# Four small reorderings at the start, at two hand-overs and in the last product of an attention and two-layer kernel

## Chip, cores and metric

One core of a Trainium2 chip runs the whole program. The metric is the device time of one execution in microseconds (us); a comparison takes the median of the runs of each kernel.

## What is computed

Causal attention over 2 batches, 12 heads, 448 positions and 64 values a head, and then two layers on its 896 x 768 result. Cut to what matters:

```python
scores = scale * q @ k.T ; scores = where(above diagonal, -1e9, scores)
attn = exp(scores - max) / (sum + 1e-9) ; x = attn @ v        # 896 x 768 after the heads are joined
g1 = sigmoid(x @ w_gate) * (x @ w_val)                        # product 1, two 768 x 1536 weights
y = g1 @ w_out                                                # product 2, 1536 x 768
h = y @ w2_in ; g2 = h * clip(h + 3, 0, 6) / 6                # product 3, 768 x 2048
out = g2 @ w2_out                                             # product 4, 2048 x 768
```

Inputs arrive as 64-bit words (weights) and 32-bit words (q, k, v); the result is 32-bit.

## The kernel before

Every factor of the four products is held as two parts, hi (rounded) and lo (what is left), and each product is the sum of three terms hi*hi, hi*lo and lo*hi on TensorE (PE). ScalarE (ACT) makes hi, VectorE (DVE) makes lo by a subtraction. Weights come as 64-bit words in units of 128 x 768: SyncE (SP) fetches them three units ahead, ACT and DVE turn them into 32-bit numbers (L115, L120, L124, L128, L134: "decode") and split them (`dec_hi` L153, `dec_lo` L158).

**Attention** works on 12 pairs of heads. Its steps are sorted by a table of due times (`AT`, `OWN`) in `emit_in_order`, so each engine gets them in that order. `load` (L248) fetches q and k of a pair as two halves of 112 KB each; all of these go through SP's queue but one: k of pair 0, which the line below sends through ACT's queue. In the table that fetch stands behind the turning out of the first transposed q.

```python
(nc.scalar if (p, nm) == (0, "k") else nc.sync).dma_start(
```

`t_pe` (L260) transposes q and k on PE, `t_out` copies them out of PSUM (q by ACT at L270, k by DVE at L272), `s_pe` (L285, L293) makes the scores, `s_max`, `s_exp`, `s_nrm`, `c_pe`, `d_pe` do the rest. 19 idle matmuls (`z_pe`, L456) on constants keep PE at work in the first microseconds; nine of them stand first on PE.

**Products 1 and 3** make their first units (eight and four) plainly with `halves` (L190, 36 matmuls of 448 columns a unit) and the rest by the class `Pairs`: for a pair of weight units it makes seven products P1 to P7 (L708, nine matmuls of 448 columns each) into three PSUM banks instead of eight, with sums of blocks made by DVE (`w_sums`). `run` writes out the order by hand. P1, P6, P7 and P4 add up in one bank (`banks[p][0]`), P5 and then P3 in a second (`banks[p][1]`). Between them ACT copies out what is there (`copy_out`, L725) and DVE adds the rest (`add_out`, L729): P4 may begin only when P7's state of bank 0 has been copied out. For all pairs but the last, P4 and P3 are put between the products of the next pair; for the last pair they stand alone at the end of `run`, P4 first. The hooks `end1` to `end3` split factors for the next product while this goes on. In product 1 the pairs end by sigmoid or a multiplication (L875, L877), in product 3 by hardswish (L1045 on ACT, L1046 on DVE).

**Product 2** (`halves`, L190) makes six blocks `py` of 128 x 896, with two units of weights each. **Product 4** (L1161, 384 columns a matmul) runs over two column halves `c`, eight steps `s` of two factors `g2[f]` (f = 0 to 15) and seven row tiles `t`; the last two steps are done together, row tile by row tile. In the first half `g2_split` splits two factors a step (ACT L1128, DVE L1129), and `advance` decodes and splits one weight unit a step; on DVE they stand in one line.

Of the kernel before, what the change touches and what calls it, by code (L numbers as in the profile page):

```python
# [8 lines left out]
F32 = mybir.dt.float32  # L9
# [22 lines left out]
def kernel(  # L32
# [12 lines left out]
    nc = tc.nc  # L45
    B, H, S, D = q.shape
# [126 lines left out]
    def acc():  # L173

        pool = psum[acc_n[0] // 2 % len(psum)]
        acc_n[0] += 1
        return pool.tile([P, 2, 512], F32, tag="m", name="m")
# [33 lines left out]
    with tc.manual_schedule():  # L211

        with ExitStack() as actx:
# [19 lines left out]
            live = {}  # L233

            def load(p, nm):
                b, hp = divmod(p, NPAIR)
                if nm == "v":
                    for j in range(2):
                        chunks = v[b, 2 * hp + j].rearrange("(c p) d -> p c d", p=D)
                        for x in range(2):  # L240
                            nc.sync.dma_start(
                                out=vs[p % NV][x * D : (x + 1) * D, x != j :, j],
                                in_=chunks[:, x != j :: 2],
                            )
                    return
                t = p_raw.tile([CP, S // CP, 2, D], F32, tag=nm, name=nm)
                for j in range(2):
                    (nc.scalar if (p, nm) == (0, "k") else nc.sync).dma_start(  # L248
                        out=t[:, :, j, :],
                        in_=(q if nm == "q" else k)[b, 2 * hp + j].rearrange(  # L250
                            "(c p) d -> p c d", p=CP
                        ),
                    )
                live[nm, p] = t
# [260 lines left out]
            def emit_in_order():  # L515
# [19 lines left out]
                for key in sorted(left, key=lambda key: (when(key), key)):  # L535
                    _, fn, args = left[key]
                    fn(*args)

            ones = nc.const_aps.tensor(1.0, [P, 512], BF16)
            idle_ps = ps_pt.tile([P, 512], F32, tag="pt", name="pt")  # L540
            make_identity(nc, identf)
# [83 lines left out]
        def w_dec():  # L625

            i = stream[0]
            stream[0] += 1
            u = order[i]
            decode_a(u)  # L630
            if i + 3 < NU:
                load_unit(order[i + 3])
            if u not in in_pairs:
                behind.append(u)

        def w_parts():
            while behind:
                u = behind.pop(0)
                (dec_dma if u < len(order1) else decode_b)(u)
# [4 lines left out]
        class Pairs:  # L644
# [110 lines left out]
            def P7_add(self, p):  # L755
                self.add_out(p, 1, "C22")

            def P4(self, p):
                self.product(self.banks[p][0], self.grp.pop((p, 4)), 0, "T4", False)

# [6 lines left out]
            def run(self, end1, end2, end3):  # L767

                for p in range(self.n):
                    end = p == self.n - 1
                    self.P1(p)
                    self.P1_out(p)
                    if p:
                        self.P7_add(p - 1)
                    if p or not self.ahead:
                        self.w_g1(p + 1)
                        w_dec()  # L780
                    self.P2(p)
                    self.w_g1_lo(p + 1)
                    self.P2_add(p)
                    if p:
                        self.P4(p - 1)
                        self.P4_out(p - 1)
                    self.P6(p)
                    self.P6_out(p)
                    if self.ahead and p == 0:
                        y_split("T4")  # L790
                    self.w_sums(p + 1)
                    if p:
                        self.P3(p - 1)
                        self.P3_add(p - 1)
                    if end:
                        end1()
                    self.w_g4(p + 1)
                    self.w_g2(p + 1)
                    self.P5(p)
                    soon = p and self.soon(p - 1)  # L800
                    if not end:
                        w_parts()
                    if soon:
                        self.finish(p - 1)
                    if not end:
                        w_dec()
                    if p and not soon:
                        self.finish(p - 1)
                    self.P7(p)
                    self.P7_out(p)  # L810
                    if end:
                        self.P7_add(p)
                        end2()
                    else:
                        self.w_g3(p + 1)
                p = self.n - 1
                self.P4(p)
                self.P4_out(p)
                self.P3(p)
                w_parts()  # L820
                end3()
                self.P3_add(p)
                self.finish(p)

        def single_banks():
            for pool in reversed(psum):
# [134 lines left out]
        g1 = {}  # L961
# [33 lines left out]

        for o in range(KD):
            py = acc()
            for s in range(2):
                halves(py, u, g1_of, 6 * s, s == 0, s == 1)
                if s == 1:  # L1000
                    for b in range(2):
                        split(y_of(0, o, b), y_of(1, o, b), py[:, b, :S])
                    if o < HK:
                        nc.scalar.copy(both(yr[o]), py[:, :, :S])
                    else:
                        (y11, y12), (t4, t3) = (
                            [yr[i][:, b * S : (b + 1) * S] for b in range(2)] for i in (o - HK, o)
                        )
                        sub(t3, py[:, 1, :S], y12)
                        sub(y12, y12, y11)  # L1010
                        add(y11, t3, y11)
                        sub(t4, py[:, 0, :S], y11)
                if 2 * o + s in (4, 6):
                    w_dec()
                w_dec()
                w_parts()
                u += 1
# [101 lines left out]
        def g2_split(*fs):  # L1119
            for f in fs:  # L1120
                if f >= K2:
                    continue
                i = 2 * f
                if i < 3 * len(homes2):
                    hi, lo = (home(homes2, i + x, "g2") for x in range(2))
                else:
                    hi, lo = tiles_of_e(i)
                nc.scalar.mul(hi, g2_raw(f), 1.0 / 6.0)  # L1128
                nc.vector.scalar_tensor_tensor(  # L1129
                    lo, g2_raw(f), 1.0 / 6.0, hi.bitcast(F32), op0=ALU.mult, op1=ALU.subtract,  # L1130
                )
                g2[f] = hi, lo
# [10 lines left out]
        third.run(  # L1143
            lambda: g2_split(0), lambda: g2_split(1), lambda: None,
        )
        g2_split(2, 3)
        w_dec()
        w_parts()
        u = stream[0] - 3
# [4 lines left out]
        for c in range(2):  # L1154
            cs = slice(c * HC, (c + 1) * HC)
            po = [None] * NTT

            def block(t, s, w):
                for i in range(2):
                    for n, (a, e) in enumerate(TERMS):  # L1160
                        nc.tensor.matmul(  # L1161
                            po[t],
                            lhsT=g2[2 * s + i][a][:, t * P : (t + 1) * P],
                            rhs=w[e][:, i * HC : (i + 1) * HC],
                            start=(s == 0 and i == 0 and n == 0),
                            stop=(s == NS - 1 and i == 1 and n == 2),
                        )

            osb = acts.tile([P, NTT, HC], F32, tag=f"r1{c}", name="osb")
            for s in range(NS - 2):  # L1170
                if c == 0:
                    g2_split(2 * s + 4, 2 * s + 5)
                for t in range(NTT):
                    if s == 0:
                        if t % 2 == 0:
                            pair = acc()
                        po[t] = pair[:, t % 2, :HC]
                    block(t, s, split_t[u])
                advance(u)
                u += 1  # L1180

            for t in (0, 2, 4, 6, 1, 3, 5):
                for i in range(2):
                    block(t, NS - 2 + i, split_t[u + i])
                if t % 2:
                    nc.vector.tensor_copy(osb[:, t], po[t])
                else:
                    nc.scalar.copy(osb[:, t], po[t])
                if t == 6:
                    advance(u)  # L1190
                if c == 1:
                    nc.sync.dma_start(out=outs[:, t, cs], in_=osb[:, t])
            advance(u + 1)
            u += 2
            if c == 0:
                nc.sync.dma_start(out=outs[:, :, cs], in_=osb)
# [31 lines left out]
```

## Time and profile before

| | us |
|---|---|
| median of three runs | 590.04 (589.8 to 591.88) |
| profiled execution, its own time | 589.66 |
| its span, first to last instruction | 587.9 |
| PE busy | 573.8 (98%) |
| DVE busy | 450.6 (77%) |
| ACT busy | 325.1 (55%) |
| attention, until product 1 has PE alone | 0 to 110 |
| product 1 | 110 to 268 |
| product 2 | 268 to 355 |
| product 3 | 355 to 465 |
| product 4 | 465 to 587 |

Busy time of a matmul includes its way through the array, so matmuls overlap and 98% does not say that PE runs at its peak; the distance between the starts of two matmuls tells the pace. What PE waited for, and where, is told by the table of waits and by the timeline.

### The profile page before, as it was taken

The numbers are of one execution on the slowest core, as the hardware profiler recorded it, in microseconds if no ns is written. First come the engines' busy times: TensorE is split into PE (matmuls) and PEld (weight loads), VectorE is DVE, ScalarE is ACT, GpSimd is POOL, SyncE is SP. The second block draws the span as 40 slices with busy tenths as digits, with TensorE's granted clock in tenths as the row PEclk, the third lists the DMA queues.
The fourth block names the chain that finished last, engine by engine and source line by source line (L and its number), as shares of the span: only waits on it lengthen the run. The fifth ranks groups of instructions, "written<-read, shape, count | busy, mean of one in ns | idle before, by whom it ended". The sixth has DMA issues, their size and how long they took to land.

```text
span 587.9 us, 8611 instructions
## 1 busy us (share of the span) xinstructions
PE 573.8 (98%) x3252; PEld 506.1 (86%) x3253; DVE 450.6 (77%) x673; ACT 325.1 (55%) x619; POOL 88.1 (15%) x146
## 2 busy tenths in 40 slices
PE   6999999999999999999999999999999999999997
PEld 3666666899998999889999999988899899899997
DVE  1778995588778889889767887898999888867601
ACT  1988986454747565577343223777776644433200
POOL 0545455012201111110000000113122000000000
PEclk7999999999999999999999999999999999999999
DMA  7645625069848776761334533577988333338002
GB/s 150 155 118 132 146 67 177 2 157 216 212 131 193 180 208 168 198 180 31 108 115 154 162 107 108 145 179 187 216 191 224 94 107 110 107 109 255 0 3 92
DMA packets 86921, 82.21 MB, mean 140 GB/s; under 512 B 35680, under 2 KB 77408, under 8 KB 86880
## 3 DMA queue, kind: packets, MB, share of 16 engines
q1 hardware_dynamic: 79904, 64.27, 37.0%
q0 software_dynamic: 6048, 17.17, 15.9%
q8 instruction: 25, 0.41, 0.3%
q10 hardware_dynamic: 928, 0.23, 0.2%
q14 instruction: 16, 0.13, 0.1%
HBM read 61.73 MB, written 2.75 MB: 110 GB/s over the span
## 4 chain that ended last, share of the span: by engine, by line
PE 55%; DVE 29%; ACT 10%; issue 4%; DMA 2%; ACTq 0%; DVEq 0%
PE m L1161 17%; PE w L708 11%; PE m L190 10%; DVE b L128 5%; PE pav L367 5%; PE s L293 4%; PE pt L347 4%; DVE b L134 4%; DVE lo L158 3%; DVE b L124 3%; ACT hi L153 2%; ACT b L115 2%; PE tr L260 2%; DVE g L182 2%; DVE raw L120 2%
## 5 line engine op out<-in xcount | busy, mean ns | idle before, releaser
L1161 PE MATMUL m<-hi,g 128*128 128x384 f32 x448 | 114.3, 335 | 0.7 <-DVE g L1129 0.7
L153 ACT CAST hi<-b 128x768 fp32r<-128x768 f32 x36 | 29.8, 836 | 104.3 <-DVE b L134 96.3
L1161 PEld LDWEIGHTS m<-hi,g 128*128 128x128 f32 x448 | 80.8, 188 | 1.5 <-DVE g L1129 1.3
L1161 PE MATMUL m<-lo,g 128*128 128x384 f32 x224 | 74.9, 335 | 0.4 <-DVE lo L158 0.4
L708 PE MATMUL w<-T,hi 128*128 128x448 f32 x252 | 72.0, 367 | 1.4 <-ACT g2r L725 1.4
L190 PE MATMUL m<-g,hi 128*128 128x448 f32 x288 | 70.1, 365 | 0.0
L128 DVE SCALAR_TENSOR_TENSOR b<-b,raw 128x768 int32<-128x768 int32 x68 | 65.3, 960 | 2.3
L134 DVE SCALAR_TENSOR_TENSOR b<-raw,b 128x768 int32<-128x768 int32 x68 | 65.3, 960 | 2.4
L115 ACT ACTIVATE b<-raw 128x768 f32<-128x768 f32 x68 | 61.3, 905 | 0.0
L190 PEld LDWEIGHTS m<-g,hi 128*128 128x128 f32 x288 | 54.1, 188 | 4.3
L124 DVE TENSOR_SCALAR b<-b 128x768 f32<-128x768 f32 x68 | 37.9, 557 | 25.7 <-ACT b L115 25.3
L158 DVE TENSOR_TENSOR lo<-b,hi 128x768 fp32r<-128x768 f32 x36 | 34.2, 956 | 27.4 <-ACT hi L153 27.2
L337 POOL TENSOR_SCALAR pr<-pr,rc 128x192 f32<-128x192 f32 (+3 forms) x96 | 46.1, 497 | 53.0 <-DVE rc L329 43.9
L708 PEld LDWEIGHTS w<-T,hi 128*128 128x128 f32 x252 | 47.1, 188 | 5.9 <-ACT g2r L725 1.8
L190 PE MATMUL m<-x,hi 128*128 128x448 f32 x192 | 49.1, 368 | 0.0
L708 PE MATMUL w<-T,lo 128*128 128x448 f32 x126 | 46.3, 368 | 0.7 <-DMA lo<-S 0.5
L317 ACT ACTIVATE pr<-s,nm 128x192 f32<-128x192 f32 (+3 forms) x96 | 44.5, 476 | 3.7 <-DVE nm L305 3.2
L144 POOL DMA_DIRECT2D lo<-S x26 | 24.9, 956 | 131.4 <-ACT lo L143 111.2
L1161 PEld LDWEIGHTS m<-lo,g 128*128 128x128 f32 x224 | 42.0, 188 | 0.7 <-DVE lo L158 0.7
L305 DVE TENSOR_REDUCE nm<-s 128x2 f32<-128x384 f32 (+3 forms) x48 | 30.7, 681 | 14.9 <-PE s L293 14.5
L190 PE MATMUL m<-g,lo 128*128 128x448 f32 x144 | 41.0, 366 | 0.0
L190 PEld LDWEIGHTS m<-x,hi 128*128 128x128 f32 x192 | 35.7, 188 | 3.1 <-issue 0.4
(127 smaller groups left out, 1054.7 us busy)
## 6 DMA issues: line engine op xcount, KB each, us to landing
raw<-in_moe_w_out_dram SPq DMA_DIRECT2D x28, 768.0 KB, 4.4
raw<-in_moe_w_in_dram SPq DMA_DIRECT2D x16, 768.0 KB, 4.7
lo<-S POOLq DMA_DIRECT2D x26, 384.0 KB, 4.2
raw<-in_moe_w_gate_dram SPq DMA_DIRECT2D x12, 768.0 KB, 5.1
raw<-in_moe_w_val_dram SPq DMA_DIRECT2D x12, 768.0 KB, 5.3
q<-in_q_dram SPq DMA_DIRECT2D x24, 112.0 KB, 2.9
g<-b POOLq DMA_DIRECT2D x7, 384.0 KB, 6.5
k<-in_k_dram SPq DMA_DIRECT2D x22, 112.0 KB, 4.0
```

The lines of the kernel that those rows point to most:

```text
L115: nc.scalar.activation(b, words(u)[0].bitcast(F32), AF.Copy, scale=REBIAS)
L124: nc.vector.tensor_scalar(b, b, UPPER_MAX, -UPPER_MAX, op0=ALU.min, op1=ALU.max)
L128: nc.vector.scalar_tensor_tensor(bi, bi, 3, words(u)[1], op0=ALU.logical_shift_left, op1=ALU.bitwise_or)
L134: nc.vector.scalar_tensor_tensor(bi, words(u)[0], -(2 ** 31), bi, op0=ALU.bitwise_and, op1=ALU.bitwise_or)
L153: nc.scalar.copy(hi, part_t[u])
L158: nc.vector.tensor_sub(lo, part_t.pop(u), split_t[u][0].bitcast(F32))
L190: nc.tensor.matmul(ps[:, b, :S], lhsT=w[a][:, i * P : (i + 1) * P], rhs=x(c, k0 + i, b), start=(first and i == 0 and n == 0), stop=(last a ...
L305: nc.vector.tensor_reduce(nm, live["s", p, t], axis=AX.X, op=ALU.max, negate=True)
L317: nc.scalar.activation(to if j else to[:, ::-1], ps[:, j].rearrange("p (c d) -> p c d", d=D), AF.Exp, bias=nm[:, j : j + 1], accum_out=sm[ ...
L337: nc.gpsimd.tensor_scalar(pr[:, j], pr[:, j], rc[:, j : j + 1], 1.0, op0=ALU.mult, op1=ALU.mult)
L708: nc.tensor.matmul(ps, lhsT=w[a][:, k * P : (k + 1) * P], rhs=x[:, c, i], start=(first and i == 0 and n == 0), stop=(i == HK - 1 and n == ...
L1161: nc.tensor.matmul(po[t], lhsT=g2[2 * s + i][a][:, t * P : (t + 1) * P], rhs=w[e][:, i * HC : (i + 1) * HC], start=(s == 0 and i == 0 and ...
```

## The change

- `load(0, "k")` is called ahead of everything else of the attention, and `load` returns at once where the tile is already there. The two halves of k of pair 0 thus become the first instructions on ACT's queue, ahead of its table load; the step in the table issues nothing any more.
- For the last pair of `run`, a new `P5_out` copies P5 out of bank 1 into C22 ahead of P7, and a new `P5_add` adds bank 0 (P1 + P6 + P7) to it by DVE after P7, in the place of `P7_out` and `P7_add`. P3 then comes ahead of P4, and `P4_out` goes behind `finish`.
- Ahead of the first block of product 2 one 32-bit matmul of 64 x 64 on a factor that is already there writes a corner of `py`, which the next matmul overwrites.
- `g2_split` makes three factors ahead of product 4 instead of two, and its steps of two go on from there.

```diff
             def load(p, nm):
                 b, hp = divmod(p, NPAIR)
+                if (nm, p) in live:
+                    return
...
+            load(0, "k")
             ones = nc.const_aps.tensor(1.0, [P, 512], BF16)
...
+            def P5_out(self, p):
+                nc.scalar.copy(self.hold(p, "C22"), self.banks[p][1])
+
+            def P5_add(self, p):
+                self.add_out(p, 0, "C22")
...
+                    if end:
+                        self.P5_out(p)
                     self.P7(p)
-                    self.P7_out(p)
                     if end:
-                        self.P7_add(p)
+                        self.P5_add(p)
                         end2()
                     else:
+                        self.P7_out(p)
                         self.w_g3(p + 1)
                 p = self.n - 1
-                self.P4(p)
-                self.P4_out(p)
                 self.P3(p)
                 w_parts()
                 end3()
                 self.P3_add(p)
+                self.P4(p)
                 self.finish(p)
+                self.P4_out(p)
...
             py = acc()
+            if o == 0:
+                t = g1[0][0].bitcast(F32)[:, :D]
+                nc.tensor.matmul(py[:D, 0, :D], lhsT=t, rhs=t, start=True, stop=True)
...
-        g2_split(2, 3)
+        g2_split(2, 3, 4)
...
-                    g2_split(2 * s + 4, 2 * s + 5)
+                    g2_split(2 * s + 5, 2 * s + 6)
```

ACT's first rows, before:

```order
L270 ACT_TABLE_LOAD
L270 ACTIVATE qt<-tr 128x448
L248 DMA k<-in_k_dram 112x4x64 x2
L270 ACTIVATE qt<-tr 128x448
L317 ACTIVATE pr,sm<-s,nm 128x3x64
```

The same rows now:

```order
L250 DMA k<-in_k_dram 112x4x64 x2
L272 ACT_TABLE_LOAD
L272 ACTIVATE qt<-tr 128x448 x2
L319 ACTIVATE pr,sm<-s,nm 128x3x64
L319 ACTIVATE pr,sm<-s,nm 128x192
```

The fetch of k moved from behind the copy of the transposed q, which waits for PE, to the front of the queue.

PE at the end of product 1, before (T_1723 is P7's factor, T_1724 P4's, x_73 P3's; `m` is product 2):

```order
L708 MATMUL w<-T_1723,lo 128x448
L708 MATMUL w<-T_1724,g 128x448 x9
L708 MATMUL w<-x_73,hi 128x448 x2
L708 MATMUL w<-x_73,lo 128x448
L190 MATMUL m<-g_2963,hi 128x448 x4
```

The same place now, from P7's last matmul:

```order
L711 MATMUL w<-T_1723,lo 128x448
L711 MATMUL w<-x_73,hi 128x448 x2
L711 MATMUL w<-x_73,lo 128x448
L711 MATMUL w<-T_1724,g 128x448 x9
L1011 MATMUL m<-g_2963 64x64
L190 MATMUL m<-g_2963,hi 128x448 x4
```

P3 stands between P7 and P4 now (its six rows of two and one matmuls are cut to the first two), and the 32-bit matmul stands ahead of product 2. The end of product 3 changes in the same way, without that matmul.

DVE from the last add of P7 or P5 in product 3 to the first decode of product 4, before (w_4526 to w_4528 are the last pair's banks, g2r_4538 and 4539 its C blocks):

```order
L729 TENSOR_TENSOR g2r_4539<-w_4527,g2r_4539 128x448
L1129 SCALAR_TENSOR_TENSOR g2_4621<-g2r_3751,g2_4592 128x896
L1046 SCALAR_TENSOR_TENSOR g2r_4539<-h_4633,w_4526 128x448
L158 TENSOR_TENSOR lo_4647<-b_4497,hi_4645 128x768
L158 TENSOR_TENSOR lo_4651<-b_4542,hi_4649 128x768
L729 TENSOR_TENSOR g2r_4538<-w_4527,g2r_4538 128x448
L1046 SCALAR_TENSOR_TENSOR g2r_4539<-h_4654,g2r_4539 128x448
L1046 SCALAR_TENSOR_TENSOR g2r_4538<-t_4657,g2r_4538 128x896
L1129 SCALAR_TENSOR_TENSOR g2_4621<-g2r_3751,g2_4621 128x896
L1129 SCALAR_TENSOR_TENSOR g2_4662<-g2r_3946,g2_4662 128x896
L120 TENSOR_SCALAR raw_4432<-raw_4432 128x768
```

And now (numbers one or two higher):

```order
L732 TENSOR_TENSOR g2r_4540<-w_4527,g2r_4540 128x448
L1143 SCALAR_TENSOR_TENSOR g2_4622<-g2r_3752,g2_4593 128x896
L158 TENSOR_TENSOR lo_4636<-b_4498,hi_4634 128x768
L158 TENSOR_TENSOR lo_4640<-b_4543,hi_4638 128x768
L732 TENSOR_TENSOR g2r_4539<-w_4528,g2r_4539 128x448
L1060 SCALAR_TENSOR_TENSOR g2r_4540<-h_4652,g2r_4540 128x448
L1060 SCALAR_TENSOR_TENSOR g2r_4539<-t_4655,g2r_4539 128x896
L1060 SCALAR_TENSOR_TENSOR g2r_4540<-h_4658,w_4527 128x448
L1143 SCALAR_TENSOR_TENSOR g2_4622<-g2r_3752,g2_4622 128x896
L1143 SCALAR_TENSOR_TENSOR g2_4663<-g2r_3947,g2_4663 128x896
L1143 SCALAR_TENSOR_TENSOR g2_4666<-g2r_3947,g2_4663 128x896
L120 TENSOR_SCALAR raw_4433<-raw_4433 128x768
```

P4's hardswish moved from the third place to the eighth, and a third split stands ahead of the decode; in the last step of the first half of product 4 one split is left where there were two.

## Rows read from the trace of the kernel before

**Rows 1.** The page: busy us of each engine, share of the span, instructions.

```profile
PE 573.8 (98%) x3252; PEld 506.1 (86%) x3253; DVE 450.6 (77%) x673; ACT 325.1 (55%) x619; POOL 88.1 (15%) x146
```

**Rows 2.** Waits of PE, longest first: us in total, times, longest us.

```profile
PE tr L260 <- DMA k<-in_k_dram: 4.6, 1, 4.6
PE w L708 <- ACT g2r L725: 2.0, 2, 1.4
...
PE m L1161 <- DVE g L1129: 0.7, 2, 0.5
```

**Rows 3.** Chain of work, first 30 us: start, us, what.

```profile
5.36 4.02 DMA k<-in_k_dram
...
9.42 1.01 PE tr L260 x4
...
12.04 1.87 PE s L293 x8
13.90 0.60 PE tr L260 x4
...
17.67 0.95 PE s L293 x8
```

**Rows 4.** Timeline: issues on SP's and ACT's queues: start us, us, engine, what.

```profile
0.74 3.06 SPq L248 DMA_DIRECT2D q<-in_q_dram  x6
...
4.87 0.99 ACTq L248 DMA_DIRECT2D k<-in_k_dram  x2
```

**Rows 5.** Fetches of the first 20 us: count, KB each, median us to landing.

```profile
q<-in_q_dram SPq DMA_DIRECT2D x12, 112.0 KB, 2.9
```

**Rows 6.** Stretches: us, busy per engine, then PE's clock, DMA share, GB/s.

```profile
3.79:7.20 3.41, 1.03 (x7) 0.46 (x5) 0.00 (x0) 0.54 (x1) 0.00 (x0) 1.00 0.89 201
7.20:10.61 3.41, 1.19 (x5) 1.00 (x6) 0.14 (x1) 0.00 (x0) 0.00 (x0) 0.50 1.00 187
```

**Rows 7.** Timeline, product 1: two runs of 18 matmuls, then P7's end and P4.

```profile
236.70 3.81 PE L708 MATMUL w<-x,g 128*128 128x448 f32 x18
...
250.33 3.88 PE L708 MATMUL w<-x,g 128*128 128x448 f32 x18
...
263.14 0.37 PE L708 MATMUL w<-T,lo 128*128 128x448 f32 x1
...
264.13 2.09 PE L708 MATMUL w<-T,g 128*128 128x448 f32 x9 [0.62 <-ACT h L725]
```

**Rows 8.** PE's groups by shape: busy us, mean ns; the smallest 32-bit one.

```profile
L293 PE MATMUL s<-kt,qt 64*128 64x64 f32 x48 | 5.0, 285 | 0.0
```

**Rows 9.** Timeline of PE and DVE from P7's end in product 3 on.

```profile
461.66 0.62 DVE L729 TENSOR_TENSOR g2r<-w,g2r 128x448 f32<-128x448 f32 x1 [0.46 <-ACT g2r L725]
461.68 2.09 PE L708 MATMUL w<-T,g 128*128 128x448 f32 x9 [0.62 <-ACT g2r L725]
462.51 1.09 DVE L1129 SCALAR_TENSOR_TENSOR g<-g2r,g 128x896 fp32r<-128x896 f32 x1 [0.23 <-ACT g L1128]
...
464.39 0.62 DVE L1046 SCALAR_TENSOR_TENSOR g2r<-h,w 128x448 f32<-128x448 f32 x1 [0.78 <-ACT h L1045]
...
465.44 0.33 PE L1161 MATMUL m<-hi,g 128*128 128x384 f32 x1
...
466.12 0.45 PE L1161 MATMUL m<-lo,g 128*128 128x384 f32 x1 [0.35 <-DVE lo L158]
```

**Rows 10.** DVE's timeline ahead of product 4's decodes.

```profile
468.49 1.09 DVE L1046 SCALAR_TENSOR_TENSOR g2r<-t,g2r 128x896 f32<-128x896 f32 x1 [0.49 <-ACT t L1045]
469.50 2.08 DVE L1129 SCALAR_TENSOR_TENSOR g<-g2r,g 128x896 fp32r<-128x896 f32 x2
471.51 0.55 DVE L120 TENSOR_SCALAR raw<-raw 128x768 int32<-128x768 int32 x1
```

**Rows 11.** PE and DVE at the last two steps of product 4's first half.

```profile
510.81 2.09 DVE L1129 SCALAR_TENSOR_TENSOR g<-g2r,g 128x896 fp32r<-128x896 f32 x2
...
512.95 0.62 PE L1161 MATMUL m<-hi,g 128*128 128x384 f32 x2 [0.21 <-DVE g L1129]
```

## The prediction

> **What bounds the kernel now.** I read the page first: PE is busy for 98% of the span [rows 1], so time is won only where PE stands still or runs at a lower pace. The table of PE's waits names the places [rows 2]: 4.6 us once for the fetch of k, 2.0 us in two stops for ACT's copies out of PSUM in the pair products, 0.7 us in two stops for DVE's splits in product 4. The reader should see that no wait there is long except the first. The chain of the first 30 us shows what that one is: after the transposes of q the chain goes through a fetch of k from 5.36 for 4.02 us, and the transposes of k start at 9.42 [rows 3]. The timelines of the two hand-overs from a pair product show PE stopped between P7 and P4 [rows 7, 9].
>
> **The early fetch of k.** ACT's two issues stand at 4.87, behind the copy of q, and take 0.99 us; SP's six q fetches begin at 0.74 [rows 4]. The new place is the front of ACT's queue, so they begin at about 0.74 and the second half goes out at 1.23. From issue to landing a q half took 2.9 us in the median [rows 5] and this k half 4.02 [rows 3]: it lands between 4.1 and 5.25. PE cannot take it before 9.42 - 4.6 = 4.82, where the q transposes end. I take 5.05, nearer to the longer row, since q and k now share the engines: 9.42 - 5.05 = 4.37 us. The ends: 4.6 (it is there at once) and 3.2 (it lands like the last of the six q halves, issued at 0.74 + 5 x 0.51 = 3.29, plus 2.9, so 6.2). ACT's table load and its first copy, which has no input before 4.82, move behind two issues of 0.5 us each: nothing waits for that.
>
> A second gain hangs on it. PE worked 1.03 us of the 3.41 us from 3.79, and the granted clock was 1.00 there and 0.50, the 1.2 GHz level, from 7.20 on [rows 6]. So the first k transposes took 1.01 us and the first scores 1.87, where the same groups take 0.60 and 0.95 at 13.90 and 17.67 [rows 3]: 0.41 + 0.92 = 1.33 us of the chain. Before it fell, PE had stood idle since 4.82. With k at 5.05 it doesn't, and I take it that the clock stays up: 1.33. It is 0 if it falls all the same, and I see no loss, since PE only gets more work there.
>
> Against that stands q of pair 1, fourth of SP's six halves: issued at 0.74 + 3 x 0.51 = 2.27, landed at 5.2. Two k halves in between push it by up to two steps of 0.51, to 6.2, and PE asks for it at 5.05 + 0.60 + 0.2 = 5.85: 0.35 us back. Together 4.37 + 1.33 - 0.35 = **5.35 us**, between 3.2 and 5.9. Behind that everything hangs on what came before it, so the shift goes through: the longer waits of PE all lie in the pair products and product 4 [rows 2], where they hang on ACT and DVE, which shift along.
>
> The Trainium skill says in DMA: Bandwidth & Descriptors, section Issuing engines are not separate DMA queues, that fetches issued by several engines run on the same 16 DMA engines and interleave, so that a second issuer saves only issue time. The trace agrees in part: from 3.79 to 7.20 the engines were 0.89 busy at 201 GB/s [rows 6], most of it for SP's fetches, as ACT's were issued from 4.87 on. By that rule alone the k halves take turns with q, and the saving would be nearer to 3.2 us; that is the first rival.
>
> **The end of product 1.** P7's last matmul starts at 263.14, P4's first at 264.13 [rows 7]. At 0.21 us a matmul PE loses 0.78 us there, for ACT's copy. Now P3 follows P7 and needs only bank 1, which ACT has copied out during P7; ACT's copies stay equal in number. P4 needs DVE's add of P7, which has P3's 1.85 us to be done in and takes about 0.6 (the same form in [rows 9]). The 32-bit matmul is new. Its price is bounded by a quarter of the four transposes in 0.60 us [rows 3], 0.15, and by twice the 0.285 us of the 64 x 64 group [rows 8], 0.6; I take that row's 0.3. Net **0.48 us**, between 0.2 and 0.65. P4's output is worked on last, but product 2 asks for these factors only in its second unit, over 7 us later.
>
> What is the matmul for? PE has two paces: 18 matmuls took 3.81 us from 236.70 and 3.88 us from 250.33 [rows 7], both at the full clock: less the 0.37 us of the last one, over 17 steps, that is 0.203 and 0.2065 us a matmul, 0.004 or 2% apart. The slower pace lasted until the stop at 264.13 and was gone after it. Without that stop it could go on; an odd matmul may break it as the stop did. In the trace all 32-bit work ends before the plain products begin, so I cannot see this there; I count no gain and no loss and keep a rival for it. [...] The rows show 203 and 206. [...]
>
> **The end of product 3 and product 4.** PE stops at 461.68 (0.62) and at 466.12 (0.35, for a lo) [rows 9]. Both go: P3 runs first, and DVE makes lo before the work on P4. But what is saved there counts only if the last split of product 4's first half comes earlier too, because PE stops for it again: it resumes at 512.95, when DVE's two splits from 510.81 are done [rows 11]. The chance to be early lies with DVE's line. Its decodes began at 471.51 [rows 10], and from there to 512.9 it does step after step. One split more stands ahead of that point (two took 2.0 us, rows 10) and one fewer at the end: zero in sum. So the gain is what DVE no longer waits ahead of 471.51: 0.46 for P7's copy, 0.23 for a hi, 0.78 for P4's hardswish [rows 9]. The 0.49 for the t of the other hardswish [rows 10] stays, as ACT can begin it only after P3's add. That is 1.47, and about 0.2 more, since the lo's no longer stand behind P4: **1.7 us**. The ends: 0, if new waits of the same size take their place (DVE now has P4's hardswish just ahead of the splits, and ACT makes three hi's behind it); and 3.0, if PE never stops: from 461.68 - 0.78 = 460.9 on 18 matmuls at 0.203 and 261 (six steps of 42 and nine) at 0.203 x 384/448 = 0.174 end at 510.0.
>
> **The sum.** 5.35 + 0.48 + 1.7 = 7.5 us. The profiled execution took 589.66, of which 1.8 lie outside the span and stay; 589.66 - 7.5 = 582.1. The median of the runs lies 0.38 above the profiled one: **582.5 us**.
>
> **Rivals.** *K comes late or the clock falls*: the front gives 3.2 instead of 5.35, so 584.7. For it speak the shared engines above; against it, that with both queues at work k's halves still landed about 4 us after their issue. *The slow pace stays through product 2*: from 264 to PE's next stop there are 432 matmuls of product 2 and 144 plain ones of product 3; 576 x 0.004 = 2.3 us, so 584.8. For it: the pace held for over 20 us once; against it: most stops in the trace were followed by the faster one. *The end of product 3 only moves its stop* to the last split: 584.2. The change would then not do there what it says. *Slower than before*: the earlier start could set PE to the slow pace from the first plain product on, and with fewer stops to break it, it could last. It decides at nearly all of the 1746 matmuls of 448 columns and 672 of 384: 7.0 + 2.3 less the 0.9 us that is in the trace already, 8.4 us, more than the gain: 590.9. Nothing in the trace speaks for so long a stretch.
>
> **How the numbers follow.** The forecast has 0.61 (580.2 to 584), the late front 0.17, the slow pace in product 2 0.09, the moved stop 0.07, the slow pace everywhere 0.02, and 0.04 is for less than 580.2 (front 5.9, end 3.0, slow stretches gone). The range 580.2 to 585.2 takes in the forecast and the three rivals just above it. A measurement of this kernel tells about 0.5% (2.95 us) from no change: faster means under 587.1. All but the last rival and two of the others at once lie there: 0.95 faster, 0.04 within, 0.01 slower.
>
> **What would show it.** Right: the transposes of k start near 5, the clock row stays at 1.00 from 7.20 on, the first scores take about 1 us; no stop between P7 and the last products of products 1 and 3; the last split of product 4's first half ends about 7.5 us earlier than 512.9, 5.8 of it from ahead. Wrong: PE waiting for q of pair 0 or 1 for over 1 us; 18 matmuls in 3.88 us in product 2; DVE's decodes of product 4 no earlier against P7's end than before; a stop of ACT's queue behind the two issues.

## The result, and the profile after

The changed kernel takes 580.97 us (median of four runs, 580.82 to 581.41) against 590.25 (589.8 to 591.88): a ratio of 0.984, 95% interval 0.982 to 0.986. The forecast was 582.5 with a range of 580.2 to 585.2. The profiled execution took 580.91 us, its span is 579.1: 8.7 us shorter than before, where 7.5 were forecast. The medians lie 9.3 us apart.

The page after (busy us, share of the span, instructions) shows PE at 99% where it was at 98% [rows 1]:

```profile
PE 570.8 (99%) x3255; PEld 505.0 (87%) x3255; DVE 450.1 (78%) x673; ACT 324.8 (56%) x619; POOL 88.7 (15%) x146
```

The table of PE's waits after (us in total, times, longest):

```profile
PE w L711 <- ACT g2r L728: 1.1, 1, 1.1
PE m L1175 <- DVE g2r L1060: 1.0, 1, 1.0
...
PE tr L262 <- DMA q<-in_q_dram: 0.4, 2, 0.2
PE w L711 <- ACT h L728: 0.4, 1, 0.4
PE tr L262 <- DMA k<-in_k_dram: 0.3, 1, 0.3
```

Against [rows 2]: the 4.6 us for k are 0.3, one of two stops for ACT's copies in the pair products is gone, and so are those for the splits. The second line is new, and the prediction had not named it: PE now waits 1.0 us in product 4 for a hardswish of DVE.

The front, from the timeline after (start us, us, engine, what; in brackets the idle time ahead and what ended it):

```profile
0.74 1.01 ACTq L250 DMA_DIRECT2D k<-in_k_dram  x2
...
4.60 0.57 PE L262 MATMUL tr<-identf,q 112*128 112x112 f32 x4 [0.24 <-DMA q<-in_q_dram]
5.01 0.55 PE L262 MATMUL tr<-identf,k 112*128 112x112 f32 x4
...
5.97 0.57 PE L262 MATMUL tr<-identf,q 112*128 112x112 f32 x4 [0.20 <-DMA q<-in_q_dram]
...
6.66 1.11 PE L295 MATMUL s<-kt,qt 64*128 64x192 f32 x8
```

and the same stretches as in [rows 6] (us, busy per engine, clock, DMA share, GB/s):

```profile
3.79:7.20 3.41, 2.97 (x30) 2.01 (x30) 0.63 (x1) 1.09 (x2) 0.00 (x0) 1.00 1.18 226
7.20:10.61 3.41, 3.10 (x30) 1.70 (x27) 2.44 (x5) 1.40 (x7) 0.00 (x0) 1.00 0.91 162
```

K's transposes start at 5.01 instead of 9.42, and the clock stays at 1.00, the 2.4 GHz level, from 7.20 on, where it was 0.50. The 8.7 us by stage, from the first instruction of each stage in the two traces: 6.0 up to the first pair of product 1, 0.9 up to product 2, nothing in product 2 and the plain units of product 3, 1.0 in the pairs of product 3, 0.8 in product 4.

### The profile page after: what moved, and what is told of

The parts are those of the page before. It is cut to its first block, busy times and chain, and to the rows that moved or that the text cites. A ratio compares the mean times of both kernels' runs of the same rounds, so it can differ in the third digit from the quotient of the medians.

```text
span 579.1 us, 8618 instructions
## 1 busy us (share of the span) xinstructions
PE 570.8 (99%) x3255; PEld 505.0 (87%) x3255; DVE 450.1 (78%) x673; ACT 324.8 (56%) x619; POOL 88.7 (15%) x146
## 4 chain that ended last, share of the span: by engine, by line
PE 60%; DVE 27%; ACT 8%; issue 3%; DMA 1%; SPq 1%; ACTq 0%; DVEq 0%; POOLq 0%
PE m L1175 20%; PE w L711 14%; PE m L190 10%; PE pav L369 5%; DVE b L128 5%; PE pt L349 4%; PE s L295 4%; DVE b L134 4%; DVE lo L158 3%; DVE b L124 2%; ACT hi L153 2%; DVE g L182 2%; ACT b L115 2%; PE tr L262 2%; DVE raw L120 1%
```

## Experiments

"Before" beside each is the kernel before on the same chip: 589.9 us for the first four, 590.07 for the next four, then 589.85 for three and 590.53 for the last. In the theories, "slow pace" is the distance of 0.2067 us between the starts of two matmuls of 448 columns, "fast" that of 0.2027.

**The early fetch alone.** Before, plus:

```diff
+                if (nm, p) in live:
+                    return
...
+            load(0, "k")
```

> The kernel before with the early fetch of k alone. Theory: the front is worth 4.4 us of waiting and 1.6 us of clock whatever stands behind it, so the last work of the attention comes 6.0 us earlier, and the time is about 584.2 us. Rival: part of the 6.0 us belongs to the other edits or is given back behind the attention; then 585 to 587 us.

Measured: 583.31 us (582.96 to 583.77), ratio 0.989 [0.988, 0.991], granted clock 1.00 from 7.20 us on. It is 6.6 us faster, a little over the theory, which holds: this part carries over two thirds of the gain. The rest of the change is worth 2.3 us by the two times, or 2.7 by the two gains over before.

**The clock without the early fetch.** Before, plus 20 idle matmuls on constants between q's and k's transposes, so that PE works while it waits for k:

```diff
+            WARM += [-80000 + i for i in range(20)]
```

> The kernel before, k fetched as late as before, with 20 more idle matmuls (about 4.3 us at the full clock) on PE between the transposes of q and those of k. Theory: the 1.6 us beyond the shift of the k transposes is the clock alone: it stays at 1.00 from 7.20 on, k's transposes stay at 9.4 us, the attention ends 1.6 us earlier, about 588.6 us. Rival: the 1.6 us come from the transfers behind k that are earlier too; then the clock stays up and the time is 590.2 us.

Measured: 590.12 us (589.37 to 594.37), ratio 1.002 [1.000, 1.004]. By the time alone the rival would have it. The trace of this run says something else. Timeline of PE and stretches:

```profile
10.10 0.61 PE L260 MATMUL tr<-identf,k 112*128 112x112 f32 x4
...
12.48 0.60 PE L260 MATMUL tr<-identf,k 112*128 112x112 f32 x4
...
178.91 0.47 PE L709 MATMUL w<-T,lo 128*128 128x448 f32 x1 [1.78 <-DMA lo<-raw]
```

```profile
7.20:10.61 3.41, 3.41 (x19) 1.68 (x18) 0.00 (x0) 0.00 (x0) 0.00 (x0) 1.00 0.86 172
...
180.00:184.00 4.00, 4.00 (x13) 3.57 (x13) 3.73 (x7) 2.09 (x4) 0.00 (x0) 0.57 0.92 252
```

The clock kept 1.00 at the front, and from k's first transposes to its second ones it took 2.4 us, against 4.4 before (9.42 to 13.84 in its timeline): the lower clock had cost 2.0 us there, not 1.33. K's fetch landed 0.7 us later, and 1.3 us of gain were left up to product 1. Then PE stood 1.78 us for a lo that POOL's DMA brought late (6.4 us from issue to landing in the median of that stretch, 4.9 before), the clock fell to half for 3.4 us behind this stop, and PE ran at the slow pace for most of products 1 to 3. Why that fetch was late here and in no other trace stays open. What the fall costs in the end is suggested by executions of the kernel before, but not shown by an edit. Of the 16 in this comparison, 4 had a mean granted clock of 0.999 or 1.0 and took 589.0 to 589.4 us; the 12 with 0.994 had a median of 590.1. That would be about 1 us of the whole time, of the 2.0 at its place. In the later comparisons 4 of 26 executions had such a clock: two took 589.1 and 589.3 us, but the other two 590.6 and 591.5, no less than the rest.

**The ends of products 1 and 3 alone.** Before, with `P5_out` and `P5_add` in the last pair, P3 ahead of P4, and `P4_out` behind `finish`, without the 32-bit matmul and the third split ahead:

```diff
-                    self.P7_out(p)
+                    if end:
+                        self.P5_out(p)
...
-                self.P4(p)
-                self.P4_out(p)
                 self.P3(p)
...
+                self.P4(p)
                 self.finish(p)
+                self.P4_out(p)
```

> The kernel before with P5 copied out ahead of P7 and P3 ahead of P4 alone, no 32-bit matmul, no split ahead. Up to P7 in product 1 it is the kernel before, where PE had the slower pace (0.2065 us a matmul) from 243 on. Theory: the stop after P7 is gone, product 2 starts 0.9 us earlier, and the slower pace goes on through product 2 and the plain units of product 3, 576 matmuls, 2.3 us more; with small gains and losses in product 4 about 591 us. Rival: the pace comes back to 0.203 by itself at the hand-over; then 588.5 us.

Measured: 587.71 us (587.23 to 588.75), ratio 0.997 [0.996, 0.998]. It lies under both, 0.8 us below the rival. Its trace shows both at work: the stops between P7 and the last products are gone, and PE came into product 2 at the fast pace, but changed over inside it (timeline of PE):

```profile
281.77 0.97 PE L190 MATMUL m<-g,hi 128*128 128x448 f32 x4
282.62 0.67 PE L190 MATMUL m<-g,lo 128*128 128x448 f32 x2
283.12 0.99 PE L190 MATMUL m<-g,hi 128*128 128x448 f32 x4
```

Two matmuls take 0.67 instead of 0.57 us, after a gap of 0.04 us, and from there on four take 0.99 instead of 0.97. That lasted until a stop at 401, some 120 us, and cost PE 2.3 us by the count of its matmuls. The whole time shows less of it, as the next run tells.

**The same with the 32-bit matmul:**

```diff
+            if o == 0:
+                t = g1[0][0].bitcast(F32)[:, :D]
+                nc.tensor.matmul(py[:D, 0, :D], lhsT=t, rhs=t, start=True, stop=True)
```

> The kernel of the run before with the 32-bit matmul ahead of product 2. Theory: it costs 0.46 us and sets PE back to 0.203 us a matmul, so product 2 takes 2.3 us less than in the run without it: about 589 us, 1.8 us under that run. Rival: the pace is set by something else; then the time is 0.5 us above that run.

Measured: 587.09 us (586.79 to 587.57), ratio 0.996 [0.994, 0.997]: 0.6 under the last one, where the theory had 1.8. Here PE came to the end of product 1 at the slow pace (18 matmuls in 3.88 us from 250.69), and behind the 32-bit matmul it ran at the fast one (four in 0.97):

```profile
250.69 3.88 PE L708 MATMUL w<-x,g 128*128 128x448 f32 x18
...
267.52 0.33 PE L1008 MATMUL m<-g 128*64 128x64 f32 x2
267.78 1.08 PE L190 MATMUL m<-g,hi 128*128 128x448 f32 x4
...
269.10 0.97 PE L190 MATMUL m<-g,hi 128*128 128x448 f32 x4
```

Product 2 and the plain units of product 3 took 116.84 us here and 118.87 in the run before. But most of these 2.0 us isn't kept. Early in the pairs of product 3 PE needs a copy of ACT, which began at nearly the same time in both (388.87 here, 388.74 there). A slower PE comes to this place later and doesn't stop (the run without the 32-bit matmul, then this one):

```profile
386.04 3.88 PE L708 MATMUL w<-y,g 128*128 128x448 f32 x18
389.76 0.57 PE L708 MATMUL w<-T,hi 128*128 128x448 f32 x2
```

```profile
384.62 3.81 PE L708 MATMUL w<-y,g 128*128 128x448 f32 x18
389.44 0.67 PE L708 MATMUL w<-T,hi 128*128 128x448 f32 x2 [1.02 <-ACT g2r L725]
```

From product 2's first matmul to this place the two runs differ by 0.9 us: that is what was left of the 2.3.

**The changed kernel without the 32-bit matmul** (the three lines above taken out):

> The changed kernel without the 32-bit matmul ahead of product 2. In the changed kernel the matmul and the restart behind it cost about 0.46 us of PE's line, and PE ran at the faster pace (0.203 us a matmul) ahead of it already. Theory: the pace stays fast without it, so this kernel is 0.4 to 0.5 us faster than the changed kernel: 580.5 against 580.97. Rival: the matmul sets or keeps the fast pace; without it product 2 or the plain products of product 3 run at 0.2067 us a matmul for a long stretch, as they did for 120 us in the kernel with the reordered ends alone: 2.3 us lost less 0.46, so about 582.8.

Measured: 581.67 us (580.97 to 583.21): 0.7 over the changed kernel, so the theory, that it only costs there, falls; the runs lie between what the two had said. In the trace the slow pace begins in product 2 again, behind a gap of 0.04 us for a lo (timeline of PE, then that of DVE's lo):

```profile
274.00 0.98 PE L190 MATMUL m<-g,hi 128*128 128x448 f32 x4
...
275.22 0.98 PE L190 MATMUL m<-g,hi 128*128 128x448 f32 x4
276.07 0.68 PE L190 MATMUL m<-g,lo 128*128 128x448 f32 x2
276.59 0.99 PE L190 MATMUL m<-g,hi 128*128 128x448 f32 x4
```

```profile
275.06 0.96 DVE L158 TENSOR_TENSOR lo<-b,hi 128x768 fp32r<-128x768 f32 x1 [0.90 <-ACT hi L153]
```

Here too PE comes to ACT's copy in the pairs of product 3 so late that it doesn't stop for it, so 0.9 us of the slow pace are left. Less the 0.3 that are saved ahead of product 2, that is 0.6 of the 0.7.

**Two ordinary matmuls in its place,** to tell the matmul's kind from its delay:

```diff
-                t = g1[0][0].bitcast(F32)[:, :D]
-                nc.tensor.matmul(py[:D, 0, :D], lhsT=t, rhs=t, start=True, stop=True)
+                for _ in range(2):
+                    nc.tensor.matmul(py[:, 0, :S], lhsT=split_t[u][0][:, :P], rhs=g1_of(0, 0, 0), start=True, stop=True)
```

> The changed kernel with two ordinary matmuls of 448 columns in the place of the 32-bit one; their result is overwritten. They take 0.41 us of PE, nearly what the 32-bit one takes (0.46). Theory: in the changed kernel, where PE came to this place at the fast pace, the 32-bit matmul helps by its delay alone: PE then comes to the first block of product 2 a little later and doesn't run into the stop of 0.04 us for a lo at 275.8 after which the kernel without it ran at 0.2067 us a matmul for 120 us. So the time is that of the changed kernel within 0.3, 580.7 to 581.3, and no slow stretch begins at 276. Rival: only a 32-bit matmul keeps PE at the fast pace; then product 2 falls to the slow pace as without it, 581.7 to 583.2.

Measured: 580.88 us (580.76 to 581.38), the time of the changed kernel, with no slow stretch up to 440 us. So in this trace, where PE arrives fast, a delay of 0.4 us by ordinary matmuls did what the 32-bit matmul does: PE reached the first block a little after its lo. Whether ordinary ones would also end a slow pace with which PE arrives was not tried.

**A second 32-bit matmul, in product 3:**

```diff
+                    if self.ahead and p == 3:
+                        t = self.form["B11"][:, 0, 0].bitcast(F32)[:, :D]
+                        nc.tensor.matmul(
+                            self.banks[p][2][:D, :D], lhsT=t, rhs=t, start=True, stop=True
+                        )
```

> The changed kernel with a second 32-bit matmul of 64 x 64, ahead of P2 of the fourth pair of product 3, where the changed kernel runs at the slow pace of 0.2067 us a matmul for 42 us. Theory: a 32-bit matmul sets PE back to 0.203 us, which is worth about 0.8 us over those 42 us, and costs 0.46: 580.6 against 580.97. Rival: a 32-bit matmul has no hold on the pace; the slow stretch stays and the cost is added: 581.4.

Measured: 581.05 us (581.01 to 581.41), no gain. The trace has 18 matmuls in 3.81 us behind it, where the changed kernel's has 3.88, so the slow stretch was absent. But this matmul did not end it: PE ran at the fast pace already in the last matmuls ahead of it (0.203 us apart from 415.85 to 416.86), and the traces with the two ordinary matmuls and with the splits moved (below), which lack this one, were fast there as well. So the experiment never met the case that it was made for. What it cost and what it gave back can't be told apart at this size.

**P4's hardswish sooner.** The changed kernel with:

```diff
-                self.finish(p)
                 self.P4_out(p)
+                self.finish(p)
```

> The changed kernel with P4's hardswish of the last pair of product 3 put back ahead of the other two hardswishes (the rest of the new order stays). Theory: the new stop of 0.95 us of PE at the third row tile of product 4 comes from the bank of P4, which is read last; with this edit the bank is free at about 459.1 against 460.7, the stop goes, and DVE no longer waits 0.55 us for the other hardswish. The last split of product 4's first half has about 0.3 us to spare now and comes some 0.3 us earlier, so 0.6 of the 0.95 stays: 580.4 against 580.97. Rival 1: the last split takes it all back, DVE being the bound: within 0.15 of 580.97. Rival 2: the whole 0.95 is kept: 580.0.

Measured: 581.21 us (580.86 to 581.75): nearest to rival 1, and rather a loss. First the stop in the changed kernel that it was to remove (PE and DVE):

```profile
460.08 0.61 DVE L1060 SCALAR_TENSOR_TENSOR g2r<-h,w 128x448 f32<-128x448 f32 x1
...
460.75 0.44 PE L1175 MATMUL m<-hi,g 128*128 128x384 f32 x1 [0.95 <-DVE g2r L1060]
```

That hardswish reads P4's PSUM bank, which the third row tile of product 4 takes over. In this experiment the third row tile did not stop, but at the end of the first half PE did (its own timeline):

```profile
502.66 0.86 PE L1175 MATMUL m<-hi,g 128*128 128x384 f32 x2
...
503.94 1.08 DVE L1143 SCALAR_TENSOR_TENSOR g<-g2r,g 128x896 fp32r<-128x896 f32 x1
504.08 0.44 PE L1175 MATMUL m<-lo,g 128*128 128x384 f32 x1 [0.55 <-DVE lo L158]
```

PE waits here for a lo that stands just ahead of the last split on DVE; it ran from 501.71 in the changed kernel and from 503.06 here, and the last split from 502.59 and 503.94. Of this, 0.55 us is not the edit's: this execution ran at the slow pace from 173 to 262 and began product 4 at 458.09 instead of 457.54. The other 0.8 is: with P4's hardswish in front, DVE waits 0.64 us for an h and 0.22 for a t at the head of its line, where it waited 0.55 for a t, and all behind it is later. The stop was handed on, and product 4 took 121.9 us against 121.6.

**Two splits ahead again instead of three:**

```diff
-        g2_split(2, 3, 4)
+        g2_split(2, 3)
...
-                    g2_split(2 * s + 5, 2 * s + 6)
+                    g2_split(2 * s + 4, 2 * s + 5)
```

> The changed kernel with two splits ahead of product 4 again instead of three. Theory: the look-ahead moves one split from the end of DVE's line to its front and is zero in sum; the last split ends at the same time (503.6 us in the trace of the changed kernel) and PE doesn't stop for it: within 0.2 of 580.97. Rival: the look-ahead is what took the stops at the end of product 4's first half away; without it PE stops there for the last two splits as before, 0.9 to 1.3 us, so 581.9 to 582.3.

Measured: 581.04 us (580.96 to 581.2), the time of the changed kernel. DVE's last two splits ran from 501.87 for 2.09 us, and ended 46.1 us after product 4's first matmul, as the last one does in the changed kernel (502.59 + 1.08, from 457.54), and PE did not stop. That part of the change is zero in sum, as the prediction had it.

**The splits inside the decode.** In the changed kernel DVE stands still in each step of product 4's first half for a hi that ACT makes:

```profile
494.86 0.96 DVE L158 TENSOR_TENSOR lo<-b,hi 128x768 fp32r<-128x768 f32 x1 [0.95 <-ACT hi L153]
495.74 2.09 DVE L1143 SCALAR_TENSOR_TENSOR g<-g2r,g 128x896 fp32r<-128x896 f32 x2
```

The experiment puts the two splits into that wait:

```diff
-                if c == 0:
-                    g2_split(2 * s + 5, 2 * s + 6)
...
-                advance(u)
+                decode_a(u + LA)
+                if c == 0:
+                    g2_split(2 * s + 5, 2 * s + 6)
+                decode_b(u + LA)
+                load_unit(u + LA + 3)
```

> The changed kernel with the two splits of each step of product 4's first half moved between the decode of the weight and its lo, so that DVE does them while ACT makes the weight's hi. In the changed kernel DVE stands 0.95 us for that hi in each of six steps. Theory: the last split then ends some 5 us earlier than 503.6, but PE did not wait for it: within 0.2 of 580.97, with the stop of 1 us at the third row tile still there. Rival: DVE's line sets the end of the half after all: 0.5 to 1 us faster, 580.0 to 580.5.

Measured: 580.86 us (580.71 to 581.26): the same time, with the stop at the third row tile still there (1.14 us at 460.85). The last split started 2.2 us sooner (500.42), not 5, as the first ones now stand behind a decode; the theory holds.

**Both edits together:**

> The same, and P4's hardswish ahead of the other two. Theory: with that hardswish early the third row tile no longer stops, and what took this gain back when it was tried alone, the wait for the last split, is gone since DVE's line ends some 4 us sooner: about 1.0 us under the changed kernel, 580.0. Rival: the stop is handed on once more, to a lo of a weight or to a split of an early step, as DVE's line starts 0.8 us later: 580.6 to 581.2.

Measured: 580.15 us (580.03 to 580.17), ratio to before 0.983 [0.982, 0.985]. On the same chip the kernel with only the splits moved took 580.86 and the one with two ordinary matmuls 580.88, and none of their runs is under 580.7: a gain of 0.7 us. Product 4, from its first matmul to the end of the span, took 120.8 us against 121.6 in the changed kernel. The theory holds but for one short stop at the third step, where PE is ahead of the split of factor 5 (weight loads, matmuls and DVE):

```profile
472.22 2.09 DVE L1143 SCALAR_TENSOR_TENSOR g<-g2r,g 128x896 fp32r<-128x896 f32 x2
...
473.36 0.30 PEld L1175 LDWEIGHTS m<-hi,g 128*128 128x128 f32 x2 [0.48 <-DVE g L1143]
473.36 0.62 PE L1175 MATMUL m<-hi,g 128*128 128x384 f32 x2 [0.16 <-DVE g L1143]
```

**One step on.** The same, with factors 5 and 6 split ahead of the first decode and each step splitting for the next but one:

```diff
-                if c == 0:
+                if c == 0 and s == 0:
-                    g2_split(2 * s + 5, 2 * s + 6)
+                    g2_split(5, 6)
...
+                    g2_split(2 * s + 7, 2 * s + 8)
```

> The kernel with the splits moved in and P4's hardswish ahead, whose trace still has one stop of 0.33 us of PE at 473.36, at the third step of product 4's first half, for the split of factor 5. Here factors 5 and 6 are split ahead of the first decode again, and each later step splits the factors of the next step but one. Theory: the stop goes and nothing takes its place: 0.3 under 580.15, 579.85. Rival: the first weight's lo, now 2 us later on DVE's line, stops PE instead: 580.2 to 580.6.

Measured: 579.94 us (579.26 to 580.36), ratio 0.982 [0.980, 0.983]. PE no longer waits for DVE in product 4, and nothing took the place of that stop; but its profiled execution ran at the slow pace from 172 to 262, its runs overlap with those of the last kernel, and it ran on another chip, so the times can't tell the 0.2 us between the two. The traces can: product 4 took 120.4 us against 120.8. Both are faster than the changed kernel.

## Why the prediction was right, point by point

The direction, the place of most of the gain and nearly its size were right. Its sum of 7.5 against 8.7 measured has errors in several terms.

- **K's start** was forecast at 5.05 and came at 5.01: 4.41 us against 4.37. That the two agree is luck. The forecast had PE wait for k's second half, but that half landed at 4.8 (issued at 1.19, plus 3.6), and PE was not ready for it: q's transposes began 0.35 later than before, as q landed later, and k's followed right behind them without a wait. The bound of 3.2, that the k halves take turns with q, is out. They did share: besides q's delay, the DMA engines moved 226 GB/s from 3.79 on where they had moved 201 [rows 6]. The Trainium skill, DMA: Bandwidth & Descriptors, section Issuing engines are not separate DMA queues, says that a second issuer saves issue time only. The trace agrees as to the sharing; here the issue was all that held k back.
- **The clock** was the term that was sized too small: 1.33, from two groups of the chain, while the idle and mask matmuls and q's second transposes between them ran at the low clock too. The filled kernel shows 2.0 us for the stretch. The forecast took 0.35 back for q of pair 1; PE waits 0.2 for it and 0.3 for k of pair 1. That makes 4.41 + 2.0 - 0.5 = 5.9. The front gave 6.0 in all, above its range of 3.2 to 5.9.
- **The end of product 1**: P3 follows P7's last matmul without a stop:

```profile
256.72 0.36 PE L711 MATMUL w<-T,lo 128*128 128x448 f32 x1
256.92 0.37 PE L711 MATMUL w<-x,hi 128*128 128x448 f32 x1
```

  so the 0.78 was had. The 32-bit matmul costs more than the 0.3 of the forecast:

```profile
258.74 1.99 PE L711 MATMUL w<-T,g 128*128 128x448 f32 x9
260.66 0.33 PE L1011 MATMUL m<-g 128*64 128x64 f32 x2
260.92 1.07 PE L190 MATMUL m<-g,hi 128*128 128x448 f32 x4
```

  From P4's start to product 2's it is 2.18 us, without it 1.83 (258.80 to 260.63 in the trace of that experiment): 0.35. The next four take 1.07 instead of 0.97, which is 0.1 more, inside product 2. The stop of before had cost 0.1 behind it too: P4's nine matmuls took 2.09 us [rows 7] and take 1.99 now. So the edit gave 0.78 + 0.1 - 0.45 = 0.43 against 0.48. The 0.9 that was measured up to product 2 has another source besides: this execution had no slow stretch there, where before had one of some 20 us [rows 7], worth 0.4 (0.78 + 0.1 - 0.35 + 0.4 = 0.93). That is not the edit's: three experiments with the same start and the same end of product 1 had such a stretch again (P4's hardswish sooner, and the last two).
- **The end of product 3 and product 4** gave 1.0 + 0.8 = 1.8 against 1.7, but the step behind the 1.7 did not set the time. DVE's line won what was said: its first decode came 10.0 us after P7's last matmul (453.62 to 463.62) instead of 10.8 (460.70 to 471.51), and with one split of 1.0 more ahead of it, 1.8 in all. The stops of [rows 9] and [rows 11] went. The forecast had PE stop for the last split again; in the changed kernel it doesn't. The prediction looked only at DVE's line and not at who waits for P4's hardswish: its move behind the other two holds a PSUM bank that product 4 needs at its third row tile, and PE waits there instead. The forecast's own end without any stop was 3.0; this stop costs 1.2 with the restart behind it, which leaves 1.8 by estimate. That the two limits lie so close together is luck; the experiments with P4's hardswish and the splits show that both are there. In the pairs of product 3 a longer slow stretch (0.3 us more) and a shorter stop for ACT (0.3 less) about cancel.
- **The rivals.** The late fetch and the falling clock did not come. The slow pace through product 2 is real, in the reordered kernel and in the one without the 32-bit matmul, but its price of 2.3 us was too high: 0.9 was left behind PE's next stop, in which the slow PE had less to wait for. It did not come in the changed kernel, and the traces suggest two reasons. In four of them (the ends with the 32-bit matmul, P4's hardswish sooner, and both last kernels) PE came slow to that matmul and left it fast; and its delay keeps PE off a gap of 0.04 us, which two ordinary matmuls did as well. The Trainium skill, TensorE: Matmul & The Clock Gate, section Back-to-back issue gap, gives columns by 2.4 GHz plus 2.5 ns for a single matmul by itself, by estimate 189 ns for 448 columns, and for a stream with weight loads 131 ns at 512 columns; it has no second pace. The streams here show 203 and 207 ns for 448 columns, so the measurement decides. The moved stop came, but at another place, the third row tile, and cost 1.2 us instead of 1.7.

## What to carry to other kernels

When a reorder frees one engine, list for every step that moves back not only what stands behind it on its engine but which buffer it still holds, and who takes that buffer next. A stop that is removed is kept as a gain only if the next thing that PE needs is early as well: moving P4's hardswish gave nothing alone, and the splits in DVE's gaps gave nothing alone, but the two together gave 0.7 us. A fetch that the first instructions need belongs at the head of a queue that is idle; the clock that doesn't fall in the meantime is part of what this is worth, and counts for all the instructions in that stretch. A loss or a gain of PE counts only as far as it reaches past the next stop: 2.0 us of slower matmuls ahead of a stop for ACT came to 0.9.

## What the runs showed that was not expected

- PE's two paces at the same granted clock of 1.00, 0.203 and 0.207 us for a matmul of 448 columns with its weight load, change over at stops and even at gaps of 0.04 us, and then hold for up to 120 us. The trace of before has the slower one from 243 to 264 and from 422 to 449; the changed kernel's from 415 to 457; those with the second 32-bit matmul and with the splits moved nowhere. A stretch of 120 us costs PE 2.3 us, of which 0.9 reached past the next stop. After stops of 0.3 to 2 us PE went on at either pace, and what decides it was not found.
- Behind one gap of 4.6 us at the front the clock fell to half in most executions, but not in all: by their mean clock, 8 of 42 executions of the same kernel went without. What the fall costs the whole time, about 1 us by the first comparison, is not settled.
- Filling that gap with idle matmuls kept the clock and won nothing in the end: what it gained by the clock, 1.3 us up to product 1, later stages lost again in that execution.
